# A pad tile below the staging and output buffers of a fused retention and token-mixing kernel

## The chip, the cores and the metric

The kernel runs on one core of one Trainium2 chip. The metric is the device time of one execution in microseconds (us); of several runs the median is given. TensorE is called PE in the profile, VectorE DVE, ScalarE ACT, GpSimd POOL, and SyncE, which issues all the transfers here, SP.

## The reference, cut to what matters

Two layers follow one another. The first is a recurrence over time, per batch (4) and head (8), with a state of 64 x 64 that fades by a constant per head. The second is a token mixer whose weights depend on the input.

```python
# q, k, v: [4, 8, 768, 64] float32
gamma = 1.0 - 2.0 ** (-5.0 - np.arange(H))
for t in range(S):                                  # S = 768
    state = gamma * state + k[:, :, t] (outer) v[:, :, t]
    y[:, :, t] = scale * q[:, :, t] @ state
x = y with heads side by side                        # [4, 768, 512]
W_tok = (x @ w_q) @ (x @ w_k).T / sqrt(64)           # per batch, 768 x 768
out = relu(W_tok @ x) @ w_out                        # [4, 768, 512] float32
```

## The kernel before, in words

Time is cut into chunks of 128 steps. Two chunks make a pair (256 steps), three pairs make a batch, and there are 12 pairs, numbered 0 to 11. Per chunk the fading is folded into q and k by a table (`ck` and `cq`, helper `decay`, L280 to L289, run as multiplications in L282), v is only cast to bf16 (`cv`, L303), q and k are transposed on PE (`trk` L309, `trq` L324), scores are made and masked (`sc` L343, `eat` L359), and the output of a chunk is the masked part (`ia` L399) plus what the running state gives (`in` L384). The state is summed in PSUM (`st` L414) and copied out (`es` L427). The mixer then transposes x (`xt` L449, copied out by `exT`), projects it (`wqk` L463), sums z over the batch (`za`, `zm`, L492), and for each pair makes `mx` (L521), a ReLU (`r` L534) and the last projection (`pj` L543), whose result `eo` (L556) copies into an output buffer `o`; `store` (L561) sends it to DRAM. A plain copy goes through L138 on ACT and L140 on DVE or POOL.

The order of all this is a list written out by hand (`ORDER`, L18 to L68). Every engine runs its own entries in that order and waits where an input isn't there: `ck.1:V` is pair 1's k on DVE, `sc.0.1@0+1` the scores of pair 0's chunk 1 in PSUM banks 0 and 1. `fill.150` at the head of the list puts 150 matmuls on a zero tile in front of the first transposition (L273, L274), `fill.36` puts 36 in front of `trq.0`; they compute nothing that is used. `WO:V` (L264) is the cast of the output weights on DVE.

Inputs are loaded on SP's queue (`load`, L149 to L163), one transfer for each of q, k and v per batch, into two sets of staging buffers. Each buffer has 128 partitions of 12288 bytes. A k or v transfer is made of 6144 rows of 256 bytes (128 partitions, 8 heads, 6 chunks), since a time step of one head has 64 float32 values; a q transfer has 3072 rows of 512 bytes, because q is loaded with two neighbouring steps on one partition (L152 to L156). The first nine transfers are issued at once, in the order k, q, v of batch 0, `wq_stage`, `wk_stage`, k of batch 1, `wout_stage`, q and v of batch 1 (L169 to L176). Batch b + 2 is loaded when the third cast out of that buffer is done (`release`, L180 to L185). `wq_stage` and `wk_stage` have 512 rows of 256 bytes, `wout_stage` has 512 rows of 2048 bytes. An output buffer has 4096 bytes on each partition, and there are six of them (`N_OUT`, L71).

SBUF tiles come from one pool and lie one behind the other in the order in which the program asks for them. Below the pool lie 16384 bytes of scratch and 128 bytes of constants, so that the pool starts at byte 16512 of each partition. The first nine tiles are the three weight stages and the six staging buffers of k, q and v; their sizes (1024, 1024, 8192 and six times 12288 bytes) are all multiples of 256. Small tables and working tiles follow; an output buffer takes its place when `eo` first asks for it.

| tile | first byte in the partition | that, modulo 256 |
|---|---|---|
| `wq_stage`, `wk_stage`, `wout_stage` | 16512, 17536, 18560 | 128 |
| `k_st0`, `q_st0`, `v_st0` | 26752, 39040, 51328 | 128 |
| `k_st1`, `q_st1`, `v_st1` | 63616, 75904, 88192 | 128 |
| `o0` to `o5` | 176832 to 209856 | 192 |
| bf16 working tiles (`ks`, `kT`, `x` and so on) | 107968 and up | 192 |

Of the kernel before, what the change touches and what calls it, by code (L numbers as in the profile page):

```python
# [9 lines left out]
FP32 = mybir.dt.float32  # L10
# [60 lines left out]
N_CAST, N_QKT, N_AT, N_S, N_X, N_XT, N_WQK, N_RELU, N_OUT = 4, 3, 6, 4, 6, 2, 8, 2, 6  # L71
# [3 lines left out]
def kernel(  # L75
# [19 lines left out]
    DM = moe_w_out.shape[0]  # L95
# [17 lines left out]
    def const(name, shape, dtype):  # L113
        return sbuf.tile([128] + shape, dtype, name=name)
# [3 lines left out]
    def buf(name, i, shape, dtype):  # L118

        if (name, i) not in made:  # L120
            made[name, i] = const(f"{name}{i}", shape, dtype)
        return made[name, i]


    duos = [psum.tile([128, 2, 512], FP32, name=f"duo{i}_ps") for i in range(2)]
# [23 lines left out]
    def load(name, b):  # L149
        src = {"k": k, "q": q, "v": v}[name]  # L150
        if name == "q":
            t = buf("q_st", b % 2, [H, NP, 2, D], FP32)  # L152
            nc.sync.dma_start(  # L153
                out=t.rearrange("p h n j d -> p (h n) (j d)"),
                in_=src[b].rearrange("h (n p j) d -> p (h n) (j d)", p=128, j=2),
            )  # L156
        else:
            t = buf(name + "_st", b % 2, [H, NCH, D], FP32)
            nc.sync.dma_start(  # L159
                out=t.rearrange("p h n d -> p (h n) d"),  # L160
                in_=src[b].rearrange("h (n p) d -> p (h n) d", p=128),
            )
        staged[name, b] = t  # L163
# [116 lines left out]
    def decay(e, p, name, shape, order, table):  # L280
        t = buf(name + "s", p % N_CAST, [2, H, D], BF16)
        ENGINES[e].tensor_tensor(  # L282
            out=t,
            in0=staged[name, p // NP][shape].rearrange(order),
            in1=table.to_broadcast([128, 2, H, D]),
            op=ALU.mult,
        )
        pairs[p][name + "s"] = t
        release(name, p)  # L289
# [333 lines left out]
```

## Time and profile before

| | us |
|---|---|
| median of 3 runs | 125.39 (124.52 to 125.45) |
| the profiled execution | 125.87 |
| its span, first to last instruction | 124.1 |

| engine | busy us | share of the span |
|---|---|---|
| PE (matmuls) | 99.0 | 80% |
| DVE | 74.5 | 60% |
| ACT | 61.4 | 49% |
| POOL | 53.7 | 43% |

1.8 us of the profiled execution lie outside the span. A row of a timeline gives the start of a run of equal instructions, how long they took together, engine, line, operation and tiles (out<-in), and in brackets how long the engine had been idle before and what ended that. A row of a table of windows gives, for one stretch of time, its length, the busy time of each engine with the number of instructions, the granted PE clock as a share of full speed, the share of the 16 DMA engines that was busy (over 1 where the records of neighbouring packets overlap), and the rate of transfer in GB/s. "PEclk", "DMA" and "GB/s" of the page cut the span into 40 equal slices of 3.1 us. Releasers are inferred: where the engine that is named had long been done, it was another, often a transfer.

### The profile page before, as it was taken

The numbers are of one execution on the slowest core, as the hardware profiler recorded it, in microseconds if no ns is written. First come the engines' busy times: TensorE is split into PE (matmuls) and PEld (weight loads), VectorE is DVE, ScalarE is ACT, GpSimd is POOL, SyncE is SP. The second block draws the span as 40 slices with busy tenths as digits, with TensorE's granted clock in tenths as the row PEclk, the third lists the DMA queues.
The fourth block names the chain that finished last, engine by engine and source line by source line (L and its number), as shares of the span: only waits on it lengthen the run. The fifth ranks groups of instructions, "written<-read, shape, count | busy, mean of one in ns | idle before, by whom it ended". The sixth has DMA issues, their size and how long they took to land.

```text
span 124.1 us, 3189 instructions
## 1 busy us (share of the span) xinstructions
PE 99.0 (80%) x1362; PEld 73.3 (59%) x1362; DVE 74.5 (60%) x97; ACT 61.4 (49%) x112; POOL 53.7 (43%) x46
## 2 busy tenths in 40 slices
PE   6998464589975697499999387899399999999940
PEld 6997363378964353366898166878256686643310
DVE  1005979997855639348987669665466944523520
ACT  5000003676243450964763796554457997567520
POOL 7405445496397592308997305989500000000000
PEclk9999999968999999959999999999958999999999
DMA  1999999599999999979999999999970421062763
GB/s 67 225 217 287 279 219 217 125 247 218 332 316 281 220 214 226 217 190 305 256 218 217 224 206 288 281 220 217 382 314 12 169 104 70 0 250 116 284 243 122
DMA packets 19020, 26.66 MB, mean 215 GB/s; under 512 B 1472, under 2 KB 13760, under 8 KB 19008
## 3 DMA queue, kind: packets, MB, share of 16 engines
q1 hardware_dynamic: 19008, 26.48, 83.3%
q8 instruction: 10, 0.16, 0.6%
q14 instruction: 2, 0.02, 0.1%
HBM read 20.19 MB, written 6.29 MB: 213 GB/s over the span
## 4 chain that ended last, share of the span: by engine, by line
SPq 58%; PE 23%; DMA 11%; issue 2%; ACT 2%; ACTq 0%
SPq L159 28%; SPq L153 18%; DMA v_st<-in_v_dram 11%; PE bank_ps L547 9%; SPq L171 7%; SPq L174 5%; PE duo_ps L547 3%; PE duo_ps L349 1%; PE bank_ps L526 1%; PE bank_ps L467 1%; PE state_ps L418 1%; PE bank_ps L390 1%; PE bank_ps L405 1%; ACT o L138 1%; ACT relu L539 1%
## 5 line engine op out<-in xcount | busy, mean ns | idle before, releaser
L282 POOL TENSOR_TENSOR ks<-k_st,fk 128x1024 bf16<-128x1024 f32 x10 | 20.8, 2100 | 20.2 <-DMA k_st<-in_k_dram 17.0
L365 DVE TENSOR_TENSOR at<-duo_ps,cmask 128x1024 bf16<-128x1024 f32 x21 | 25.1, 1217 | 6.3 <-PE duo_ps L349 6.2
L282 POOL TENSOR_TENSOR qs<-q_st,fq 128x1024 bf16<-128x1024 f32 x10 | 19.8, 2005 | 6.1 <-DMA q_st<-in_q_dram 6.1
L547 PE MATMUL bank_ps<-wout_sb,relu 128*128 128x512 bf16 x72 | 19.7, 403 | 0.1
L547 PEld LDWEIGHTS <-relu 128*128 128x128 bf16 x96 | 8.3, 100 | 9.7 <-issue 2.3
L274 PE MATMUL bank_ps<-warm 128*128 128x128 bf16 x191 | 13.1, 238 | 1.0 <-DVE warm L190 1.0
L274 PEld LDWEIGHTS <-warm 128*128 128x128 bf16 x194 | 13.0, 109 | 1.1 <-DVE warm L190 1.0
L138 ACT CAST x<-bank_ps 128x512 bf16<-128x512 f32 x18 | 10.4, 589 | 4.5 <-PE bank_ps L405 4.2
L138 ACT CAST s_sb<-state_ps 64x256 bf16<-64x256 f32 x28 | 10.3, 367 | 4.5 <-PE state_ps L418 4.2
L349 PE MATMUL duo_ps<-qT,kT 64*128 64x128 bf16 x192 | 9.7, 232 | 2.5 <-ACT at L138 1.5
L418 PE MATMUL state_ps<-vs,ks 128*128 128x128 bf16 x80 | 8.6, 236 | 3.8 <-ACT vs L138 3.7
L138 ACT CAST vs<-v_st 128x1024 bf16<-128x1024 f32 x7 | 7.1, 1044 | 8.8 <-DMA v_st<-in_v_dram 8.8
L138 ACT COPY o<-bank_ps 128x512 f32<-128x512 f32 x13 | 7.6, 586 | 7.5 <-PE bank_ps L547 7.5
L138 ACT COPY qT<-bank_ps 128x1024 bf16<-128x1024 bf16 x2 | 2.0, 1012 | 16.7 <-PE bank_ps L330 16.7
L330 PE MATMUL bank_ps<-identity,qs 128*128 128x128 bf16 x80 | 6.3, 223 | 4.9 <-ACT relu L539 2.3
L541 DVE TENSOR_SCALAR relu<-bank_ps 128x512 bf16<-128x512 f32 x8 | 5.4, 689 | 8.0 <-PE bank_ps L526 8.0
L330 PEld LDWEIGHTS <-qs 128*128 128x128 bf16 x96 | 5.6, 98 | 7.7 <-POOL qs L282 3.5
L282 DVE TENSOR_TENSOR ks<-k_st,fk 128x1024 bf16<-128x1024 f32 x2 | 4.1, 2076 | 9.1 <-DMA k_st<-in_k_dram 9.1
L349 PEld LDWEIGHTS <-kT 64*128 64x128 bf16 x192 | 6.6, 100 | 4.8 <-issue 3.8
L418 PEld LDWEIGHTS <-ks 128*128 128x128 bf16 x80 | 5.9, 106 | 5.8 <-issue 4.9
L140 DVE COPY qT<-bank_ps 128x1024 bf16<-128x1024 bf16 x8 | 5.5, 688 | 6.3 <-PE bank_ps L330 5.2
L313 PE MATMUL bank_ps<-identity,ks 128*128 128x128 bf16 x80 | 6.2, 220 | 3.8 <-POOL ks L282 2.9
(75 smaller groups left out, 170.9 us busy)
## 6 DMA issues: line engine op xcount, KB each, us to landing
out_dram<-o SPq DMA_DIRECT2D x11, 512.0 KB, 2.6
wout_stage<-in_moe_w_out_dram SPq DMA_DIRECT2D x1, 1024.0 KB, 11.9
out_dram<-o SPq DMA_DIRECT2D x2, 256.0 KB, 2.3
wq_stage<-in_moe_w_q_dram SPq DMA_DIRECT2D x1, 128.0 KB, 11.1
wk_stage<-in_moe_w_k_dram SPq DMA_DIRECT2D x1, 128.0 KB, 3.2
k_st<-in_k_dram SPq DMA_DIRECT2D x4, 0.2 KB, 14.1
q_st<-in_q_dram SPq DMA_DIRECT2D x4, 0.5 KB, 14.9
v_st<-in_v_dram SPq DMA_DIRECT2D x4, 0.2 KB, 14.9
```

Of the source, the lines that this page charges most:

```text
L138: nc.scalar.copy(out=out, in_=in_)
L153: nc.sync.dma_start(out=t.rearrange("p h n j d -> p (h n) (j d)"), in_=src[b].rearrange("h (n p j) d -> p (h n) (j d)", p=128, j=2),)
L159: nc.sync.dma_start(out=t.rearrange("p h n d -> p (h n) d"), in_=src[b].rearrange("h (n p) d -> p (h n) d", p=128),)
L171: nc.sync.dma_start(out=wq_stage, in_=moe_w_q.rearrange("(a p) h -> p a h", p=128))
L174: nc.sync.dma_start(out=wout_stage, in_=moe_w_out.rearrange("(a p) m -> p a m", p=128))
L274: nc.tensor.matmul(out=ps[:, 0:128], lhsT=warm, rhs=warm, start=True, stop=True)
L282: ENGINES[e].tensor_tensor(out=t, in0=staged[name, p // NP][shape].rearrange(order), in1=table.to_broadcast([128, 2, H, D]), op=ALU.mult,)
L330: nc.tensor.transpose(ps[:, :, hp, j, :], pairs[p]["qs"][:, j, 2 * hp : 2 * hp + 2, :].rearrange("p x d -> p (x d)"), identity,)
L349: nc.tensor.matmul(out=ps[:, x, hp, :], lhsT=st["kT"][rows(x), c, hp, :], rhs=st["qT"][rows(x), c, hp, :], start=(hp == 0), stop=(hp == HP ...
L365: nc.vector.tensor_tensor(out=t.rearrange("p x hp t -> p (x hp) t"), in0=ps.rearrange("p x hp t -> p (x hp) t"), in1=cmask.rearrange("p o ...
L418: nc.tensor.matmul(out=state_ps[:, hp, :], lhsT=st["ks"][:, c, 2 * hp : 2 * hp + 2, :].rearrange("p x d -> p (x d)"), rhs=st["vs"][:, c, 2 ...
L547: nc.tensor.matmul(out=ps, lhsT=st["relu", a // 2][:, a % 2, j], rhs=wout_sb[:, a, :], start=(a == 0), stop=(a == NDM - 1),)
```

## The change

A tile `pad` of 224 float32 values (896 bytes on each partition) that nothing reads or writes is asked for first, and then the six output buffers; the staging tiles come after them. `eo` finds its buffer already made.

```diff
@@ -122,6 +122,12 @@
         return made[name, i]
 
 
+
+    const("pad", [224], FP32)
+    for i in range(N_OUT):
+        buf("o", i, [2, DM], FP32)
+
+
     duos = [psum.tile([128, 2, 512], FP32, name=f"duo{i}_ps") for i in range(2)]
```

By the same arithmetic the output buffers now start at 16512 + 896 = 17408 = 68 x 256, and the staging tiles at 17408 + 6 x 4096 = 41984 = 164 x 256. Every tile behind them moves as well, by 25472 bytes where no output buffer lay ahead of it before, and in each case by an odd multiple of 128; the bf16 working tiles are then at 64 modulo 256. No instruction, no transfer, no engine, no order and no wait is added, removed or moved.

## The prediction

> **What bounds the kernel now.** I first read the page's 40 slices, to see which resource is full in which part.
>
> ```profile
> PE   6998464589975697499999387899399999999940
> ...
> PEclk9999999968999999959999999999958999999999
> DMA  1999999599999999979999999999970421062763
> GB/s 67 225 217 287 279 219 217 125 247 218 332 316 281 220 214 226 217 190 305 256 218 217 224 206 288 281 220 217 382 314 12 169 104 70 0 250 116 284 243 122
> ```
>
> The DMA engines are at 9 from the second slice to the thirtieth, that is to some 90 us, and mostly idle afterwards; PE has gaps up to there and is at 9 behind it. So there are two stages: up to the landing of the last input the transfers set the pace, and then some 35 us are PE's. In the first stage the rate isn't constant: it sits near 218, near 285, and now and then above 310 GB/s. I read windows that hold one kind of transfer each, by SP's timeline: v of batch 2, q of batch 2, the output weights, and a burst of stores.
>
> ```profile
> 57.50:60.00 2.50, 2.50 (x49) 2.04 (x46) 2.50 (x4) 1.49 (x5) 2.50 (x3) 1.00 1.05 288
> 62.00:67.00 5.00, 5.00 (x99) 4.66 (x96) 3.53 (x7) 3.09 (x5) 5.00 (x3) 1.00 1.11 219
> ...
> 33.40:34.40 1.00, 0.95 (x20) 0.79 (x16) 0.92 (x2) 0.00 (x0) 1.00 (x1) 1.00 1.03 360
> 89.50:91.50 2.00, 1.39 (x22) 1.19 (x23) 0.52 (x1) 2.00 (x5) 0.10 (x1) 0.73 1.02 414
> ```
>
> One of 16 engines therefore needs 16 x 256 / 219 = 18.7 ns for a 256-byte row of v, 16 x 512 / 288 = 28.4 ns for a 512-byte row of q, 91 ns for a 2048-byte row of weights and 158 ns for 4096 bytes of output. The first two differ by 9.7 ns for 256 bytes more, which leaves 9.0 ns that a row costs whatever its length. That line gives 87 and 164 ns for the two longer rows, near the 91 and 158 seen. The stores' 414 GB/s show that it isn't the engines' data rate that holds k and v to 219: half of such a row's time is the 9.0 ns.
>
> **The change part by part.** It moves addresses only, so all that can change is the time of a row in a transfer, and of an engine's access to a tile. For the second I take nothing: no instruction changes its shape, type or stride, tiles that began at 128 or 192 modulo 256 now begin at 0 or 64, and the trace before holds tiles at both 128 and 192 with no sign of a price (bounds: none that a row gives, either way). What a row costs at an aligned address the trace doesn't show, because no transfer in it is aligned on the SBUF side. I bound it from the rows above: at the least nothing is saved, at the most all 9.0 ns. I take the value that a half-used block would have. A 256-byte row that starts 128 bytes into a 256-byte block touches two blocks, a 512-byte row three; if the half block that isn't wanted costs a transfer's time, that is 128 bytes at 9.7 ns per 256, or 4.8 ns a row, whatever the row's length. It fits inside the 9.0 ns that are there to be explained, and it lies in the middle of the bounds.
>
> So a k or v load (6144 rows, 384 per engine) gets 384 x 4.8 = 1.9 us shorter, a q load (192 per engine) 0.9, `wq_stage` and `wk_stage` together 0.3, `wout_stage` 0.2. As the DMA engines never pause, leads add up from load to load: k of batch 0 lands 1.9 us earlier, q 2.8, v 4.7; k of batch 1 6.8, the output weights 7.0, q 7.9, v 9.8; v of batch 2 14.4; k of batch 3 16.3, q 17.2, v 19.1. The queue doesn't hold this up: the last load needs `cv.3` to `cv.5`, of which ACT's two, quoted below, end at 49.69 + 1.99 = 51.68 and POOL's earlier, while SP issued it at 74.27.
>
> ```profile
> 74.27 3.81 SPq L159 DMA_DIRECT2D v_st<-in_v_dram  x1
> ```
>
> A lead is worth only as much as somebody waits. I went through the engines' timelines for each place where PE, or the engine that feeds it, stood still for a landing, and asked what is late next.
>
> ```profile
> 10.68 4.07 DVE L282 TENSOR_TENSOR ks<-k_st,fk 128x1024 bf16<-128x1024 f32 x2 [9.08 <-DMA k_st<-in_k_dram]
> 14.66 1.87 DVE L140 COPY kT<-bank_ps 128x1024 bf16<-128x1024 bf16 x3
> 17.23 4.07 DVE L282 TENSOR_TENSOR qs<-q_st,fq 128x1024 bf16<-128x1024 f32 x2 [0.69 <-DMA q_st<-in_q_dram]
> ...
> 35.64 2.20 DVE L140 CAST wout_sb<-wout_stage 128x2048 bf16<-128x2048 f32 x1 [1.28 <-DMA wout_stage<-in_moe_w_out_dram]
> 37.76 0.68 DVE L140 COPY xT<-bank_ps 128x1024 bf16<-128x1024 bf16 x1
> ```
>
> ```profile
> 1.04 10.46 PE L274 MATMUL bank_ps<-warm 128*128 128x128 bf16 x150 [1.04 <-DVE warm L190]
> ...
> 38.50 0.61 PE L467 MATMUL bank_ps<-xT,wq_sb 128*128 128x256 bf16 x4 [1.06 <-ACT kT L138]
> ...
> 50.79 0.38 PE L418 MATMUL state_ps<-vs,ks 128*128 128x128 bf16 x4 [2.02 <-ACT vs L138]
> ...
> 70.24 0.38 PE L418 MATMUL state_ps<-vs,ks 128*128 128x128 bf16 x4 [1.72 <-ACT vs L138]
> ...
> 77.90 0.62 PE L313 MATMUL bank_ps<-identity,ks 128*128 128x128 bf16 x8 [1.04 <-POOL ks L282]
> ...
> 83.99 0.62 PE L330 MATMUL duo_ps<-identity,qs 128*128 128x128 bf16 x8 [0.42 <-POOL qs L282]
> ...
> 90.11 0.77 PE L330 MATMUL bank_ps<-identity,qs 128*128 128x128 bf16 x8 [2.31 <-ACT relu L539]
> ```
>
> ```profile
> 49.69 1.99 ACT L138 CAST vs<-v_st 128x1024 bf16<-128x1024 f32 x2 [3.57 <-DMA v_st<-in_v_dram]
> ...
> 69.14 1.99 ACT L138 CAST vs<-v_st 128x1024 bf16<-128x1024 f32 x2 [2.49 <-DMA v_st<-in_v_dram]
> ...
> 88.52 1.04 ACT L138 CAST vs<-v_st 128x1024 bf16<-128x1024 f32 x1 [2.72 <-DMA v_st<-in_v_dram]
> ```
>
> Start: DVE's casts of k move by 1.9 us and its 0.69 us of idleness ahead of q goes, 2.6 together (q lands 2.8 earlier, which suffices). PE's 150 idle matmuls end at 11.50, so the first transposition gains less than half a microsecond; but its result waits until DVE is through with both casts, at 12.9, so this cover holds. Batch 0, weights: `WO` stands ahead of `exT.2` on DVE, and PE waits for that at 38.50. Without its 1.28 us `exT.2` comes right after; I count 1.2. Batch 1's v: `cv.3` can follow ACT's work at 46.1, and PE's 2.02 us go. Batch 2's v: `cv.6` can follow at 66.7, and 1.7 go. Batch 3's k: 1.0; POOL's `ck.10` then waits for its buffer, free when PE ends `st.6.1` at 73.5, still 2.4 us ahead of its present 75.9. Batch 3's q: 0.4. Batch 3's v: the relu that PE waits for at 90.11 stands behind `cv.11` on ACT, which waited 2.72 us; 2.3 go. The sum is 2.6 + 1.2 + 2.0 + 1.7 + 1.0 + 0.4 + 2.3 = 11.2 us. It is far less than the 19.1 of lead, and the cover is PE's own work: behind these waits the first stage becomes PE's and DVE's too. The 35 us behind `cv.11` stay as they are; of the stores only the last lies on the path, and it has 16 rows per engine at most, under 0.1 us.
>
> Because leads exceed the waits, the saving per row hardly matters: with 9.0 ns only the start gains some 0.5 more, since its idle matmuls then stand in the way (114.2); with 2.4 ns the last landing has 9.5 us of lead, and that is the gain (116.4). Below that it falls in proportion, to nothing. Made against the profiled execution, 125.87 - 11.2 = 114.7 us. The median of the runs shown lies 0.5 lower; the forecast stays with the profiled execution.
>
> **The rivals.** *The 9.0 ns don't depend on the address.* For it: one constant fits rows from 256 to 4096 bytes, the stores too, whose SBUF side lies at 192 and not at 128 and which would waste more per row; they are 6 ns faster than the line and not slower. Against it: nothing but that the constant is as large as nearly two half blocks. Then the time is that of before, 125.4 to 125.9. [...] No transfer of the trace is aligned, so none can say it yet.
>
> *Rows of 256 bytes are held by their number.* The v window passes 16 / 18.7 = 0.86 rows per ns, the q window 16 / 28.4 = 0.56. If 0.86 is a ceiling, k and v stay as they are and only q gains 0.9 us a load. Leads are then 0.9 at the first q, 2.0 at batch 1's v (with the weights), 2.8 at batch 2's and 3.7 at the last, and as each is less than the waits behind it, the last is the gain: 122.2 us. For it: the k and v windows are flat at one value. Against it: the same straight line in size fits them and longer rows alike. [...]
>
> *PE's clock gives the gain back, and more.* Place: 24.5 to 88.5 us, where PE would get denser.
>
> ```profile
> 25.00:30.00 5.00, 4.70 (x72) 4.20 (x72) 4.28 (x6) 3.52 (x6) 4.72 (x5) 0.66 1.10 233
> ...
> 24.50:49.70 25.20, 20.09 (x265) 14.61 (x265) 18.12 (x24) 10.93 (x19) 17.44 (x12) 0.93 1.07 256
> 49.70:69.10 19.40, 17.25 (x275) 13.84 (x275) 13.53 (x17) 11.74 (x22) 12.24 (x7) 0.91 1.01 234
> 69.10:88.50 19.40, 15.03 (x256) 12.44 (x256) 13.41 (x17) 12.10 (x23) 12.28 (x7) 1.00 1.07 250
> ```
>
> The three batches hold 52.4 us of PE work at a mean clock of 0.95, and the least dense of them has the full clock. The change would leave 55.4 us for them, 95% busy. At clock c the work takes 52.4 x (1/c - 1/0.95) longer; that eats 11.2 + 1.3 us from c = 0.77 downwards, and at 0.75 the kernel takes 129.4 us. For it: 0.66 has been seen in a dense window. Against it: 62 to 67 us, with PE at 5.00 of 5.00, has 1.00, and so have the fully packed slices near the end.
>
> **How the numbers follow.** My forecast has a chance of 0.58, the constant that doesn't care about addresses 0.26, the ceiling on rows 0.09, the clock 0.07. The forecast's own range is 112.5 to 118.5: 114.2 to 116.4 from the price of a row, widened by some 2 us on either side, about one of the waits above, because a wait that goes can uncover another, and because the gaps on PE that remain may shrink too. Forecast and ceiling leave more than 0.2 outside, so the range has to take in the unchanged time: 112.5 to 126.2. Faster by over 1%, about what a measurement of this kernel can tell from no change, are the first and the third case, 0.67; within 1% the second, 0.26; slower the last, 0.07.
>
> **What would show it.** Right: windows with k or v alone at 256 x 16 / 13.9 = 295 GB/s in place of 219, with q alone at 512 x 16 / 23.6 = 347 in place of 288; the DMA slices empty from about 70 us on instead of 90; `cv.3`, `cv.6` and `cv.11` on ACT no longer released by a transfer; PE's waits of 2.02, 1.72 and 2.31 us gone, and the same 35 us behind `cv.11`. Wrong: 219 and 288 as before would mean that a row's constant has nothing to do with the address; 219 with a faster q the ceiling on rows; faster loads and a PE clock under 0.8 in the middle the clock; and faster loads with a gain much under 9 us would mean that I misjudged which waits the landings end.

## The result, and the profile after

| | before | after |
|---|---|---|
| median us | 125.41 (4 runs, 124.52 to 125.45) | 110.27 (4 runs, 109.46 to 110.72) |
| profiled execution, us | 125.87 | 110.53 |
| its span, us | 124.1 | 108.7 |

The ratio is 0.88, with a 95% interval of 0.873 to 0.887. The prediction was 114.7 us with a range of 112.5 to 126.2: the direction was right, and so was the address as the cause, but the gain was larger than the range allowed, 15.1 us in place of 10.7. Medians and ranges here take in every run; a ratio compares only the runs within 1.5% of the fastest of their kernel. The lines of the slices that answer to those of before:

```profile
PE   6999984669997679999999899999999999999920
...
PEclk9999999995999999999999999999999999999995
DMA  1989995599999979699998899798013220444472
GB/s 19 320 266 346 353 337 148 154 328 236 383 390 344 330 233 332 193 369 342 301 319 258 284 347 304 241 409 344 18 71 128 111 87 0 193 193 193 193 295 91
```

A slice is 2.7 us here. The DMA engines are full up to the 28th slice, at some 76 us, where it was the 30th, at some 93; 18 of these slices lie above 300 GB/s where 5 of those did, and of three dips of PE's clock inside its work one is left. The same kinds of transfer, one to a window (v of batch 2, q of batch 2, the output weights, a burst of stores; the columns are those of before):

```profile
51.00:54.00 3.00, 3.00 (x63) 2.63 (x60) 2.76 (x4) 2.00 (x5) 2.52 (x2) 1.00 1.12 338
...
46.50:49.50 3.00, 3.00 (x41) 1.81 (x36) 3.00 (x4) 2.54 (x6) 2.47 (x2) 1.00 1.01 368
...
27.60:29.20 1.60, 1.33 (x26) 1.22 (x24) 1.12 (x2) 0.96 (x2) 0.69 (x1) 1.00 1.05 380
...
70.80:72.50 1.70, 1.70 (x30) 1.58 (x29) 0.80 (x2) 0.64 (x2) 1.70 (x2) 1.00 1.05 417
```

By the prediction's arithmetic a 256-byte row takes 16 x 256 / 338 = 12.1 ns (before 18.7), a 512-byte row 22.3 (28.4), a 2048-byte row 86 (91), and 4096 bytes of output 157 (158). By these windows the three kinds of load save 5 to 7 ns a row, and the stores 1. What a row of k, v or q costs beside its bytes falls from 9.0 to 12.1 - 10.2 = 1.9 ns.

The records of single packets bound this reading. A packet of k or v holds 1024 bytes, that is four rows, and took 79.4 ns on average before and 54.4 after; one of q, 2048 bytes and four rows too, 114.8 and 93.1. A packet of `wq_stage` or `wk_stage` is a single row of 256 bytes, and took 18.2 ns both times. For the single rows of the output weights the median fell from 88 to 84 ns and the mean rose from 96.5 to 107.4, so that no saving is shown for them. Whether the price belongs to a row or to a packet of four rows, no run here separates.

The three places at which ACT had waited for v, and PE's matmuls behind them:

```profile
43.23 1.99 ACT L144 CAST vs<-v_st 128x1024 bf16<-128x1024 f32 x2
...
59.10 1.99 ACT L144 CAST vs<-v_st 128x1024 bf16<-128x1024 f32 x2
...
74.28 1.05 ACT L144 CAST vs<-v_st 128x1024 bf16<-128x1024 f32 x1
```

```profile
35.87 0.61 PE L473 MATMUL bank_ps<-xT,wq_sb 128*128 128x256 bf16 x4 [1.24 <-DVE xT L146]
...
45.49 0.39 PE L424 MATMUL state_ps<-vs,ks 128*128 128x128 bf16 x4
...
48.80 1.04 PE L553 MATMUL bank_ps<-wout_sb,relu 128*128 128x512 bf16 x4
...
60.91 0.39 PE L424 MATMUL state_ps<-vs,ks 128*128 128x128 bf16 x4
...
66.78 0.61 PE L319 MATMUL bank_ps<-identity,ks 128*128 128x128 bf16 x8
...
76.25 0.62 PE L336 MATMUL bank_ps<-identity,qs 128*128 128x128 bf16 x8
```

No bracket stands behind them any more but the first: the waits are gone. Against the rows of before, PE is ahead by 2.6 us at `wqk.2` (38.50 before), 5.3 at `st.3.0` (50.79), 9.3 at `st.6.0` (70.24), 11.1 at `trk.10` (77.90), 13.9 at the last transposition of q (90.11) and 15.4 at the end (124.1 to 108.7). `cv.11`, the first cast of the last v on ACT, starts at 74.28 against 88.52, 14.2 us earlier; the remaining 1.2 us come from behind it, where 35.6 us have become 34.4.

At the projection of 48.80 (56.24 before) PE's lead has grown from 5.3 to 7.4 us. These 2.1 us are not among the waits that the prediction had counted. The rows of PE in the kernel before and, in the second fence, the row of after that answers to 52.55:

```profile
52.22 0.40 PE L349 MATMUL duo_ps<-qT,kT 64*128 64x128 bf16 x8 [0.49 <-ACT o L138]
52.55 1.62 PE L547 MATMUL bank_ps<-wout_sb,relu 128*128 128x512 bf16 x4
...
56.24 1.04 PE L547 MATMUL bank_ps<-wout_sb,relu 128*128 128x512 bf16 x4
```

```profile
46.59 1.04 PE L553 MATMUL bank_ps<-wout_sb,relu 128*128 128x512 bf16 x4
```

From one projection to the other it took 56.24 - 52.55 = 3.7 us before and 48.80 - 46.59 = 2.2 after: 1.5 us, and that stretch ran at half clock before. Another 0.5 is PE's wait for a copy of `o`, which ACT could make only after the late casts of v. The kernel before, cut along the periods of 3.41 us in which its clock changes:

```profile
49.46:52.87 3.41, 1.60 (x30) 1.20 (x30) 1.46 (x2) 3.14 (x6) 1.04 (x1) 1.00 1.11 217
52.87:56.28 3.41, 3.41 (x32) 2.22 (x31) 1.33 (x2) 2.26 (x5) 0.12 (x1) 0.50 0.74 207
66.52:69.94 3.42, 2.00 (x39) 1.53 (x37) 2.95 (x3) 0.93 (x2) 1.55 (x2) 1.00 0.96 225
69.94:73.35 3.41, 2.21 (x42) 1.73 (x42) 1.92 (x2) 3.41 (x7) 0.33 (x1) 1.00 1.11 217
87.00:90.42 3.42, 1.10 (x20) 0.93 (x19) 1.35 (x2) 1.90 (x3) 1.69 (x2) 1.00 1.01 386
90.42:93.83 3.41, 3.41 (x30) 1.91 (x28) 2.63 (x3) 1.46 (x4) 0.00 (x0) 0.50 0.58 237
```

Where a wait for v left PE busy for 1.60 or 1.10 us of a period, the whole next period ran at 0.50; where it left 2.00 and 2.21, because the gap fell across two periods, it ran at 1.00. Two of the waits thus had a price of their own behind them, by an estimate from these rows up to half of 3.4 us of PE work each.

### The profile page after: what moved, and what is told of

It is laid out like the page before. It is cut to its first block, busy times and chain, and to the rows that moved or that the text cites. A ratio compares the mean times of both kernels' runs of the same rounds, so it can differ in the third digit from the quotient of the medians.

```text
span 108.7 us, 3189 instructions
## 1 busy us (share of the span) xinstructions
PE 95.0 (87%) x1362; PEld 72.7 (67%) x1362; DVE 74.4 (68%) x97; ACT 61.2 (56%) x112; POOL 52.6 (48%) x46
## 4 chain that ended last, share of the span: by engine, by line
PE 69%; DVE 18%; ACT 6%; issue 2%; DVEq 0%; ACTq 0%
PE bank_ps L553 14%; PE bank_ps L280 11%; PE duo_ps L553 5%; PE bank_ps L473 5%; PE duo_ps L355 5%; PE state_ps L424 4%; PE bank_ps L411 4%; PE bank_ps L396 4%; DVE at L371 4%; DVE qs L288 4%; PE bank_ps L532 3%; PE bank_ps L336 3%; DVE wout_sb L146 3%; PE bank_ps L460 3%; PE bank_ps L319 2%; DVE kT L146 2%
## 5 line engine op out<-in xcount | busy, mean ns | idle before, releaser
L288 POOL TENSOR_TENSOR ks<-k_st,fk 128x1024 bf16<-128x1024 f32 x10 | 19.9, 2004 | 14.7 <-PE state_ps L424 6.6
L553 PE MATMUL bank_ps<-wout_sb,relu 128*128 128x512 bf16 x72 | 18.2, 380 | 0.1
L280 PE MATMUL bank_ps<-warm 128*128 128x128 bf16 x191 | 14.0, 247 | 1.0 <-DVE warm L196 1.0
L280 PEld LDWEIGHTS <-warm 128*128 128x128 bf16 x194 | 13.8, 113 | 1.0 <-DVE warm L196 1.0
L355 PE MATMUL duo_ps<-qT,kT 64*128 64x128 bf16 x192 | 8.8, 219 | 2.7 <-ACT at L144 1.5
L355 PEld LDWEIGHTS <-kT 64*128 64x128 bf16 x192 | 6.0, 94 | 5.0 <-issue 3.7
L545 ACT ACTIVATE relu<-bank_ps 128x512 bf16<-128x512 f32 x13 | 7.6, 604 | 1.8 <-PE duo_ps L553 0.7
L411 PE MATMUL bank_ps<-vs,at 128*128 128x64 bf16 x176 | 8.6, 198 | 0.0
L411 PEld LDWEIGHTS <-at 128*128 128x128 bf16 x192 | 7.9, 101 | 0.3 <-DVE at L371 0.2
L473 PE MATMUL bank_ps<-xT,wq_sb 128*128 128x256 bf16 x44 | 6.6, 273 | 1.7 <-DVE xT L146 1.5
```

The lines of the kernel that those rows point to most:

```text
L280: nc.tensor.matmul(out=ps[:, 0:128], lhsT=warm, rhs=warm, start=True, stop=True)
L288: ENGINES[e].tensor_tensor(out=t, in0=staged[name, p // NP][shape].rearrange(order), in1=table.to_broadcast([128, 2, H, D]), op=ALU.mult,)
L355: nc.tensor.matmul(out=ps[:, x, hp, :], lhsT=st["kT"][rows(x), c, hp, :], rhs=st["qT"][rows(x), c, hp, :], start=(hp == 0), stop=(hp == HP ...
L411: nc.tensor.matmul(out=st["y", c][:, h * D : (h + 1) * D], lhsT=st["at", c][:, x, hp, :], rhs=st["vs"][:, c, h, :], start=(first and h == ...
L473: nc.tensor.matmul(out=ps[:, 0 : 2 * C].rearrange("p (j c g) -> p j c g", j=2, c=2), lhsT=wq_sb[:, a].rearrange("p o h -> p (o h)"), rhs=s ...
L545: nc.scalar.activation(out=dst, in_=st["mx"][half], func=ACT.Relu)
```

## The experiments

The theory after the result: a load whose rows start off a 256-byte boundary in SBUF pays some 6.5 ns a row, a fixed price; nothing else in the change matters; and a wait of PE costs its length and, in some cases, a period at half clock. The first four kernels ran beside one another, with the kernel before at 125.25 us.

**Staging alone.** 128 bytes ahead of the staging tiles and 128 behind them, so that output buffers and working tiles stay at 192 modulo 256.

```diff
+    const("pad", [32], FP32)
     duos = [psum.tile([128, 2, 512], FP32, name=f"duo{i}_ps") for i in range(2)]
...
+    const("pad2", [32], FP32)
     warm = const("warm", [128], BF16)
```

> Only the nine staging tiles move, from 128 to 0 modulo 256; output buffers and working tiles keep 192. Theory (a load whose rows start off a 256-byte boundary in SBUF pays about 6.5 ns per row, and nothing else in the change matters): all of the gain, ratio 0.88, some 110 us; v alone at about 338 GB/s, q near 370. Rival (the output buffers or the working tiles bring part of it): clearly above 0.88, up to 125 us.

Measured: 110.23 us (4 runs, 108.04 to 110.8). A window with v alone:

```profile
53.30:56.00 2.70, 2.70 (x59) 2.43 (x56) 2.35 (x4) 2.25 (x4) 2.70 (x3) 1.00 1.11 333
```

333 GB/s, as in the changed kernel. All of the gain lies in the staging tiles.

**Output buffers alone.** As the change, and 128 bytes more between the output buffers and the staging tiles.

```diff
         buf("o", i, [2, DM], FP32)
+    const("pad2", [32], FP32)
```

> Only the output buffers move, from 192 to 0 modulo 256; staging stays at 128, working tiles at 192. Theory: nothing, 125.4 us within 1%, v alone at 219 GB/s, stores of 4096 bytes as before. [...]

Measured: 125.62 us (10 runs), ratio 1.002 (0.997 to 1.008). In its rows k and v run at the old rate, and a burst of stores is no faster than the 414 GB/s of before:

```profile
51.00:56.00 5.00, 4.46 (x67) 3.04 (x65) 4.22 (x5) 4.16 (x10) 0.00 (x0) 1.00 1.10 222
```

```profile
90.90:92.50 1.60, 1.27 (x25) 1.09 (x26) 0.72 (x2) 1.60 (x4) 0.00 (x0) 1.00 1.00 407
```

So a load that writes SBUF off the boundary pays (222 GB/s here, 333 with staging on the boundary), and a store that reads it pays next to nothing: a packet of 4096 bytes took 161 ns at the median in the four kernels with the output buffers at 192 (before, staging alone, and two further down) and 159 in the ten with them at 0.

**Other distances from the boundary.** In the same place 64 bytes (staging at 64 modulo 256) and 192 bytes (at 192).

```diff
         buf("o", i, [2, DM], FP32)
+    const("pad2", [16], FP32)      # the other kernel: [48]
```

> As the changed kernel, but the staging tiles start at 64 modulo 256. Theory of a fixed price for any start off the boundary: 125 us again, v alone at 219 GB/s. Rival (the bytes between the boundary and the start are paid for): half the price of 128, 3.3 ns a row, v alone near 266 GB/s, some 113 us.

> As the changed kernel, but the staging tiles start at 192 modulo 256. Theory of a fixed price: 125 us, v alone at 219 GB/s. Rival (the bytes ahead are paid for): one and a half times the price of 128, 9.8 ns a row, v alone near 187 GB/s; the last landing would be 13 us later than at 128 and the time about 138 us.

Measured: 125.28 us (2 runs, 124.34 and 126.22) at 64, 126.13 (2 runs, 124.71 and 127.56) at 192. Windows of k and v at 64 and, in the second fence, at 192:

```profile
50.00:55.00 5.00, 4.67 (x66) 3.01 (x66) 4.63 (x6) 4.63 (x10) 0.24 (x1) 1.00 1.11 219
```

```profile
84.00:89.00 5.00, 5.00 (x89) 4.41 (x87) 3.41 (x6) 2.08 (x3) 5.00 (x3) 1.00 1.13 223
```

The first cast of the last v on ACT, in the same order (88.52 us before):

```profile
88.94 1.04 ACT L145 CAST vs<-v_st 128x1024 bf16<-128x1024 f32 x1 [3.08 <-DMA v_st<-in_v_dram]
```

```profile
90.24 1.04 ACT L145 CAST vs<-v_st 128x1024 bf16<-128x1024 f32 x1 [2.93 <-DMA v_st<-in_v_dram]
```

Three distances, one price: over all packets of k and v the mean is 79.5 ns at 64, 79.4 at 128 and 80.1 at 192, against 54.4 at 0. A price for the bytes between the boundary and the start would have given 266 and 187 GB/s, 113 and 138 us. It falls, and with it the half-used block by which the prediction had sized the saving. What the fixed price is made of stays open. One whole further block a row would not depend on the distance either, but by the slope of the aligned rows it would be 22.3 - 12.1 = 10.2 ns, more than the 6.6 and 6.1 seen.

The next four ran beside one another, with the kernel before at 125.49 us.

**q alone.** 128 bytes on either side of each q staging tile.

```diff
+            buf("qpad", b % 2, [32], FP32)
             t = buf("q_st", b % 2, [H, NP, 2, D], FP32)
+            buf("qend", b % 2, [32], FP32)
```

> The kernel before with the two q staging tiles alone on a 256-byte boundary (128 bytes of padding on either side of each); k, v and the weights stay at 128. Theory (6.3 ns saved per q row, 1.2 us per q load; a lead is worth the waits that it meets and no more): leads of 2.4, 3.7 and 4.9 us at the v of batches 1, 2 and 3; the gain is the last lead, 4.9 us, so 120.4 us, and v alone stays at 219 GB/s. Rival (a start-up latency per load and not a price per row): no more than some 1 us, 124.4.

Measured: 120.78 us (4 runs, 119.73 to 121.1), ratio 0.966 (0.957 to 0.976). The v casts on ACT:

```profile
45.23 1.99 ACT L138 CAST vs<-v_st 128x1024 bf16<-128x1024 f32 x2 [0.87 <-DMA v_st<-in_v_dram]
64.63 1.99 ACT L138 CAST vs<-v_st 128x1024 bf16<-128x1024 f32 x2 [1.75 <-DMA v_st<-in_v_dram]
83.54 1.04 ACT L138 CAST vs<-v_st 128x1024 bf16<-128x1024 f32 x1 [2.08 <-DMA v_st<-in_v_dram]
```

They are 4.5, 4.5 and 5.0 us ahead of those of before, so the last lead and the gain are as expected; the first is larger than the 2.4 worked out, so the loads don't get ahead in equal steps. The packets of q took 95.7 ns on average (114.8 before), those of k and v 75.9 (79.4). As long as all three casts still wait for a landing, the last lead is the gain.

**PE's gaps in the kernel before, filled.** The new step puts matmuls on the zero tile into a PSUM bank that is free at the time. They compute nothing that is used.

```diff
+    def idle(e, at, n):
+        for _ in range(n):
+            nc.tensor.matmul(out=bank(at[0])[:, 0:128], lhsT=warm, rhs=warm, start=True, stop=True)
...
-    eo.1.0:V st.3.0
+    eo.1.0:V idle.32@5 st.3.0
...
-trq.11@5 cv.9:A
+idle.36@6 trq.11@5 cv.9:A
```

> The kernel before, with idle matmuls on the zero tile in PE's two longest gaps: 32 ahead of st.3.0 (gap of 2.0 us) and 36 ahead of trq.11 (gap of 2.3 us). Loads and waits stay. Theory (a gap makes PE's clock fall to half for a following window of 3.4 us, so that a wait costs more than its length): no half clock behind these two gaps, 122 to 124 us against 125.3. Rival (the half-clock windows come by themselves or with dense work): 125.3 us or more.

Measured: 124.89 us (10 runs), ratio 0.999 (0.995 to 1.003). The clock behaved as the theory said, the time didn't:

```profile
52.00:56.00 4.00, 3.95 (x56) 2.75 (x51) 3.96 (x4) 2.95 (x8) 0.29 (x1) 1.00 1.07 234
90.00:94.00 4.00, 3.44 (x47) 2.24 (x48) 2.88 (x4) 3.43 (x8) 0.00 (x0) 1.00 0.59 227
```

Both stretches have 1.00 (before 0.50). But with loads at the old pace `cv.11` still starts at 88.8 us, on the landing; ACT only waits longer for it, 3.11 us in place of 2.72, and another period at half clock came behind the next wait for v, at 72.3 us. The clock in the middle is worth something only once the loads are out of the way. That doesn't cover the second gap, behind which no load is waited for: the span of the profile is 1.2 us shorter (122.9 against 124.1), and the ratio of the runs doesn't show it. The runs of the kernel before reach from 123.73 to 126.5 us, those of this one from 124.52 to 125.53; whether all of the former had the dip behind 90 us, no trace says.

**A wait put back into the changed kernel, empty and filled.** Four ACT copies, whose result isn't used, ahead of `cv.3`; in the second kernel 44 idle matmuls ahead of `st.3.0` as well.

```diff
+    def dl(e, at, n):
+        for _ in range(n):
+            nc.scalar.copy(out=junk, in_=wout_stage.rearrange("p a m -> p (a m)")[:, 0:1024])
...
-pj.1.0@4 cv.3:A
+pj.1.0@4 dl.4 cv.3:A
...
-    eo.1.0:V st.3.0          # the second kernel alone
+    eo.1.0:V idle.44@5 st.3.0
```

> The changed kernel with four extra ACT copies of 1024 columns (some 1.0 us each, result unused) ahead of cv.3, so that PE has to wait some 2.7 us for the first v of batch 1 although it has landed. Theory (a wait costs its length, and a window at half clock on top): 113.0 us plus up to 1.7, and a window with the clock at half right behind the gap. Rival (length only): 113.0 us at most.

> As the run with the ACT delay, and PE's gap is filled with 44 idle matmuls (some 2.4 us). Theory: the clock stays at 1.00 behind the gap, and the kernel is 1 to 1.7 us faster than with the gap left empty, near 113 us. Rival: the same as with the empty gap.

Measured: 114.22 us (4 runs, 112.9 to 115.85) with the empty gap, 113.42 (4 runs, 111.45 to 113.97) with the filled one. The gap and what follows, empty first, then filled:

```profile
46.50:49.40 2.90, 0.06 (x1) 0.00 (x0) 1.19 (x2) 2.87 (x4) 1.76 (x1) 0.99 0.97 346
49.40:52.70 3.30, 3.07 (x31) 2.13 (x32) 1.63 (x2) 2.61 (x5) 0.00 (x0) 0.50 0.95 264
```

```profile
46.50:48.60 2.10, 1.85 (x39) 1.68 (x38) 0.00 (x0) 2.10 (x3) 1.17 (x1) 1.00 1.02 380
48.60:52.00 3.40, 2.86 (x47) 1.92 (x45) 2.36 (x2) 3.15 (x8) 0.67 (x1) 1.00 1.09 350
```

The same delay of the same instruction, and the clock behind it is 0.50 with PE idle and 1.00 with PE kept busy. That the gap sets the clock is shown. The times differ by 0.8 us in that direction, less than the 1 to 1.7 expected, and their ranges overlap, so the runs alone only make the price in time likely. The two traces put it at the same size: from `cv.3` to `cv.6` on ACT it took 64.48 - 48.32 = 16.2 us with the empty gap and 62.15 - 46.81 = 15.3 with the filled one, and from there to the end 49.6 in both. The other 1.5 us between their spans (114.1 and 111.8) lie ahead of `cv.3`, where the first had three periods at half clock and the second had a single one. So the period behind the gap cost 0.8 us here, less than half its length; that other engines set the pace for the rest is argued, not tried.

**Can the changed kernel be bettered?** Four kernels beside one another, with the kernel before at 125.77 us: the change again; 45 idle matmuls in PE's gaps between 16 and 24 us; the cast of the output weights on ACT; both.

```diff
-trq.1@5 trq.2@6
+idle.16@5 trq.1@5 idle.6@6 trq.2@6
...
-sc.1.1@0+1
+idle.14@4 sc.1.1@0+1
...
-sc.2.1@0+1
+idle.9@4 sc.2.1@0+1
...
-WO:V trk.5@4 ew.1:A          # the third and the fourth kernel
+WO:A trk.5@4 ew.1:A
```

> The changed kernel again, beside the next three on one chip: 110.3 us, and at least one window of the clock at half between 18 and 28 us.

> The changed kernel with 45 idle matmuls in the gaps of PE between 16 and 24 us (16 and 6 ahead of the second and third transposition of q, 14 and 9 ahead of two score blocks). Theory (a window of 3.4 us in which PE is busy for about half or less is followed by one at half clock): no half clock from there on up to the end of PE's work, 109.3 us. Rival (dense work or chance sets the clock): 110.3 us and a half-clock window as before.

> The changed kernel with the cast of the output weights on ACT in place of DVE, at the same place of the order. Theory (PE's 1.24 us ahead of wqk.2 are now DVE's cast in front of exT.2, and no longer a landing): the gap goes to 0.3 or less, 109.4 us. Rival (DVE or POOL set that stage anyway): 110.3 us.

> Both edits together, on top of the change: 108.4 us if they add up; 109.3 if they take the same time away twice.

Measured: 109.49 (6 runs, 107.26 to 111.18), 109.75, 109.64 and 109.47 us. None of them is better than the change. The first one's clock had no dip at all this time, against what was expected, and the filled one's had none either, while the kernel with the cast on ACT alone had three periods in a row at half clock, from 19.0 to 29.3 us. The periods run on their own (one begins 1.7 us after the first instruction in the trace of before, 0.2 us in that of the result), and whether a gap falls into one or across two differs between executions. `wqk.2`'s gap did go, and that brought nothing. The last v's cast in the change again shows why:

```profile
73.14 1.05 ACT L144 CAST vs<-v_st 128x1024 bf16<-128x1024 f32 x1 [0.66 <-DMA v_st<-in_v_dram]
```

and in the kernel with both edits:

```profile
71.96 1.04 ACT L144 CAST vs<-v_st 128x1024 bf16<-128x1024 f32 x1 [0.17 <-DMA v_st<-in_v_dram]
```

In these executions ACT again waits for the last landing, if by less. In the profile of the result it didn't (74.28, without a bracket). Loads and compute have come so close that either can be the later by a microsecond or two, and an edit that serves one of them alone gains nothing that shows.

## Why the prediction was right, and where it was wrong

*What bounds the kernel, and that the address decides a row's price*: right, shown by the two kernels that move staging and output buffers alone. The rival of a constant that doesn't care about addresses is out. The stores, 6 ns below the line of the loads, were read as speaking for it. They say nothing on it: by the line that the loads have now (1.9 ns and 10.2 for every 256 bytes) 4096 bytes would take 165 ns, and they take 157, so neither line holds for transfers that read SBUF.

*4.8 ns saved per row*: inside the bounds, too small by over a quarter for k and v. It was 6.6 for them, 6.1 for q, and none is shown for `wq_stage`, `wk_stage` and the output weights, for which the prediction had 0.5 us. The reason given, half a block, was an estimate, and it was wrong: the price doesn't depend on the distance (79.5, 79.4 and 80.1 ns a packet of k and v at 64, 128 and 192 bytes).

*A ceiling on the number of rows*: out; rows of 256 bytes now pass at 338 GB/s, 16 / 12.1 = 1.3 per ns against 0.86.

*"As the DMA engines never pause, leads add up"*: this was wrong too, on the other side. At the measured price 8 x 384 x 6.6 + 4 x 192 x 6.1 ns make 25 us of lead at the last landing, with the predicted one 19.1. The last packet of v ended at 88.1 us in the trace of before and at 71.4 in that of the result: 16.7 us. By the cast that waits for it, it was 88.52 - 73.14 = 15.4 and 88.52 - 71.96 = 16.6 in two of the last four kernels, and 14.1 (74.47) in the one with idle matmuls alone. That 19.1 came near is luck: a saving that was too small, times a stream that was taken to be without holes. The faster stream has holes, as the digits of 5 to 8 among the DMA slices show, where there were few but 9s; two of them:

```profile
43.70:45.00 1.30, 1.30 (x13) 0.83 (x12) 1.30 (x3) 1.30 (x2) 0.00 (x0) 1.00 0.28 68
59.00:60.40 1.40, 1.40 (x32) 1.05 (x29) 1.10 (x2) 1.40 (x3) 0.95 (x1) 1.00 0.38 97
```

```profile
38.46 5.55 SPq L159 DMA_DIRECT2D q_st<-in_q_dram  x1
44.47 2.73 SPq L165 DMA_DIRECT2D v_st<-in_v_dram  x1
...
53.93 5.39 SPq L159 DMA_DIRECT2D q_st<-in_q_dram  x1
59.77 3.30 SPq L165 DMA_DIRECT2D v_st<-in_v_dram  x1
```

Both lie where SP ends one transfer's instruction and starts the next. In both traces the first packet of batch 2's q starts some 0.8 us after SP's instruction for it has ended (54.83 and 54.03 before, 44.81 and 44.01 after); before, the transfer ahead still had packets to move until 55.3, and after it is nearly through by then. That the queue's hand-over makes the holes is argued from these places, not tried.

*The sum of 11.2 us*: this is the step that failed, and it put the time outside the range. Each wait was taken to cost its own length, and everything between the waits and behind `cv.11` to stay as it was. Up to `st.3.0` the sum was even too large: it has 2.6 + 1.2 + 2.0 = 5.8 us there, and PE is ahead by 5.3. Two rows of DVE after:

```profile
14.86 4.07 DVE L288 TENSOR_TENSOR qs<-q_st,fq 128x1024 bf16<-128x1024 f32 x2
...
32.33 2.89 DVE L146 CAST wout_sb<-wout_stage 128x2048 bf16<-128x2048 f32 x1
```

The start brought 17.23 - 14.86 = 2.4 us for the 2.6. The 1.2 of the weights hardly came: their cast no longer waits, but took 2.89 us in place of 2.20, and a gap of 1.24 us stayed in front of `wqk.2`, where PE is 2.6 us ahead and not 3.8. `st.3.0` then brought 2.7 for 2.0.

What the sum doesn't have comes behind that. Of the 2.1 us between `st.3.0` and the projection at 48.80, 1.5 come from work that had run at 0.50 and now runs at 1.00, and 0.5 from ACT's late copy. From there to the last transposition of q, PE gains 13.9 - 7.4 = 6.5 us where the sum has 1.7 + 1.0 + 0.4 + 2.3 = 5.4; these 1.1 us have no single cause that I can name. From that transposition to the end it is another 15.4 - 13.9 = 1.5 us, again a period at half clock that is gone, where the prediction held that the 35 us "stay as they are". So 11.2 - 0.5 + 2.1 + 1.1 + 1.5 = 15.4. Had the two periods, 3.0 us, stayed, the profiled execution would by this estimate have taken 110.53 + 3.0, some 113.5 us, inside the range.

This share of the clock is read from the profiled executions. The mean clock of each run is known, and doesn't go with its time: of the four runs of the changed kernel the one with the lowest, 0.951, was the fastest, 109.46 us. A period at half clock didn't cost the same everywhere: 0.8 us behind the delayed `cv.3`, and 1.5 in the tail behind `cv.11`.

The tail makes the clearest case, since no landing can cover it. From `cv.11` to the end it took 35.6 us in the kernel before, 124.5 - 88.94 = 35.6 with staging at 64 and 125.8 - 90.24 = 35.6 with staging at 192, each with a clock dip right behind 90 us; it took 123.5 - 89.48 = 34.0 with the output buffers alone moved and 122.9 - 88.81 = 34.1 with the gaps filled, neither with a dip there, and 34.1 to 34.4 in the changed kernel's two profiles. The same holds for all fourteen traces: 35.5 to 35.7 us in the four with such a period, 34.0 to 34.5 in the ten without. A period at half clock costs 1.5 us there.

*The clock as a rival*: its sign was wrong. I weighed that a denser PE loses its clock; the runs show that an emptier one does. The rows for that were in the prediction's own fences: its waits of 2.02 and 2.31 us stand directly ahead of the dips of the slices. The gap needn't fill a period of 3.41 us: 2.0 us that left PE 1.60 us of work in one were enough for 0.50 in the next.

*The range*: its lower end rested on "some 2 us, about one of the waits" for what a vanished wait might uncover. That allowed a wait to be worth less than its length, and hardly that it could be worth more.

## What to carry to other kernels

Where many short rows are loaded into SBUF, look up the address of the destination tile: 128 bytes of padding ahead of the staging tiles were worth 12% here (110.23 us against 125.25), and padding ahead of buffers that transfers only read brought nothing in the time (125.62). When a wait is removed, count beside its length what ran slowly behind it, by cutting the profile along the periods of the clock; and count it only as far as no other wait takes it up, as in the kernel whose filled gaps brought nothing. Once leads exceed waits, a further saving on the loads, or a further gap filled, has to be judged against the other side, which is then a microsecond away.

## What the runs showed of the hardware that was not expected

The price of a start off a 256-byte boundary is the same at 64, 128 and 192 bytes (79.5, 79.4 and 80.1 ns a packet of k and v on average, 54.4 without it), and lies on loads that write SBUF. It is 6.1 to 6.6 ns a row by the rates of k, v and q, whose packets are written as four rows each. Packets of a single row show none of it: 18.2 ns before and after for 256 bytes. Stores of 4096 bytes out of buffers at 192 and at 0 modulo 256 differ by 2 ns of 161.

PE's clock is set in periods of 3.41 us that are not tied to the program: one begins 1.7 us after the first instruction in the trace of before, 0.2 us in that of the result. In the fourteen traces, a period at full clock in which PE was busy for 1.40 us or less was followed by one at half clock in 17 of 17 cases (five of them behind the last matmul), one with 2.00 or more in none of 356, and one in between in 16 of 35. So the same program can have such a period or not: of the changed kernel's two profiles one has a period at half clock inside PE's work, from 24.1 us, and the other has none.
